# Attention backward for one cached token: outputs written over K and V, deeper pools, split head-0 columns, and weight reloads on another queue

## Chip, cores, metric

One core of one Trainium2 chip. A profile has its own span, about 2 us under the device time of the same run. The engines are PE (matrix products), DVE (vector), ACT (scalar), POOL (GpSimd) and SP, which here does nothing but issue DMAs. A DMA's data moves in packets on 16 DMA engines. dK, dV, dWo and dWq are the gradients of K, V, wo and wq.

## The reference, cut to what matters

The program is a forward pass and all its gradients. One token x (640 numbers) goes through an attention over a cached K and V (32 heads, 4096 positions, 128 wide) and through a small MLP, and a gate mixes the two.

```python
q = (x @ wq)                                   # 640 -> 32 heads x 128
p = softmax(einsum(q, k_cache) * Dh ** -0.5)   # per head, 4096 scores
a = einsum(p, v_cache) @ wo
b = mish(x @ w1 + b1) @ w2
out = g * a + (1 - g) * b                      # g = sigmoid(sum(x * gate_w))
# returned: out and the gradients of x, k_cache, v_cache, wq, wo, w1, b1, w2, gate_w
```

The gradients of K and V are outer products, as large as K and V. For each head the kernel reads 1 MiB of K and 1 MiB of V and writes 1 MiB of dK and 1 MiB of dV. With the weights and their gradients it reads 82.03 MB and writes 82.03 MB.

## The kernel before

The main loop has one `period` per head. SP issues all loads, POOL all large stores, each engine's own instructions run in program order.

```python
KB, VB = 4, 4
kv_in = ctx.enter_context(tc.tile_pool(name="kv_in", bufs=KB))
outs = ctx.enter_context(tc.tile_pool(name="outs", bufs=5))    # dK and dV
...
def load_k(h):                                 # load_v alike, bufs=VB
    kts[h] = kv_in.tile([P, J, Dh], BF16, name="Kn", tag="Kn", bufs=KB)
    nc.sync.dma_start(kts[h][:], Kv[h])
def load_wq(w):                                # two heads' groups, 1.25 MiB, two buffers
    wqs[w] = wts.tile([P, RC, WG * Dh], BF16, name="wq_g", tag="wq_g")
    nc.sync.dma_start(wqs[w][:], wq_v[:, :, w * WG * Dh:(w + 1) * WG * Dh])
def load_wo(g):                                # one group of four heads, 640 KiB, three buffers
    wos[g] = wts.tile([P, G, D], BF16, name="wo_g", tag="wo_g", bufs=3)
    nc.sync.dma_start(wos[g][:], wo_v[g])
...
load_wq(0); load_wo(0); load_k(0); load_v(0); load_k(1); load_v(1); load_wo(1)
# w1, b1, load_k(2), load_v(2), load_w2(0), load_w2(1)
...
def dwo():                                     # dWo is written over wo, then stored
    for i in range(G):
        nc.vector.tensor_scalar(wos[g][:, i, :], da_bc[:], fs["o4"][:, i:i + 1], None, ALU.mult)
    nc.gpsimd.dma_start(dwo_v[g], wos[g][:])
...
for h in range(H):
    hh, g = h % G, h // G
    if hh == 3:
        load_wo(g + 2)      # its buffer is free when group g-1's dWo store has landed
        if g % 2 == 0:
            load_wq(g // 2 + 1)
    load_k(h + 3)
    load_v(h + 3)
    if hh == 1 and g + 1 < NG:
        prep_steps(g + 1, h)          # q, dO and their columns for the next four heads
    period(h)
```

For head 0, `prep_steps(0, 0)` ran whole before the first score: q from wq, dO from wo, then the columns of both in one small matmul.

Of the kernel before, what the change touches and what calls it, by code (L numbers as in the profile page):

```python
# [10 lines left out]
F32 = mybir.dt.float32  # L11
BF16 = mybir.dt.bfloat16
# [4 lines left out]
def kernel(  # L17
# [24 lines left out]
    nc = tc.nc  # L42
    P = 128
    _, H, Sk, Dh = A_k_cache.shape
# [4 lines left out]
    G = 4  # L49
# [31 lines left out]
    out1_rows = out_1.rearrange("a b (c p) -> (a b c) p", p=P)  # L81
    out9_rows = out_9.rearrange("(c p) -> c p", p=P)

    KB, VB = 4, 4
    const = ctx.enter_context(tc.tile_pool(name="const", bufs=1))
    kv_in = ctx.enter_context(tc.tile_pool(name="kv_in", bufs=KB))
    outs = ctx.enter_context(tc.tile_pool(name="outs", bufs=5))
    tsb = ctx.enter_context(tc.tile_pool(name="tsb", bufs=4))
    wts = ctx.enter_context(tc.tile_pool(name="wts", bufs=2))
    small = ctx.enter_context(tc.tile_pool(name="small", bufs=3))  # L90
# [14 lines left out]


    vec_rows = const.tile([3 * RC, P], BF16, name="vec_rows")
    nc.scalar.dma_start(vec_rows[0:RC, :], x_rows)
    nc.scalar.dma_start(vec_rows[RC:2 * RC, :], dy_rows)
    nc.scalar.dma_start(vec_rows[2 * RC:3 * RC, :], gw_rows)  # L110

    kts, vts, wqs, wos = {}, {}, {}, {}

    def load_k(h):
        if h < H:
            kts[h] = kv_in.tile([P, J, Dh], BF16, name="Kn", tag="Kn", bufs=KB)
            nc.sync.dma_start(kts[h][:], Kv[h])
# [6 lines left out]
    def load_wq(w):  # L124
        if w < H // WG:
            wqs[w] = wts.tile([P, RC, WG * Dh], BF16, name="wq_g", tag="wq_g")
            nc.sync.dma_start(wqs[w][:], wq_v[:, :, w * WG * Dh:(w + 1) * WG * Dh])

    def load_wo(g):
        if g < NG:  # L130
            wos[g] = wts.tile([P, G, D], BF16, name="wo_g", tag="wo_g", bufs=3)
            nc.sync.dma_start(wos[g][:], wo_v[g])

    w2cs = {}

    def load_w2(c):
        w2cs[c] = mlp.tile([FP, FCC, D], BF16, name="w2c", tag="w2c", bufs=2)
        nc.sync.dma_start(w2cs[c][:], w2_v[:, c * FCC:(c + 1) * FCC, :])

    load_wq(0)  # L140
    load_wo(0)
    load_k(0)
    load_v(0)
    load_k(1)
    load_v(1)
# [6 lines left out]
    load_v(2)  # L152
    load_w2(0)
    load_w2(1)


    ident_f = const.tile([P, P], F32, name="ident_f")
# [79 lines left out]
    gps = {}  # L237
    steps, done = [], {}

    def add(name, kind, fn, deps=(), head=0):  # L240
        steps.append((name, kind, fn, tuple(deps), head))

    slot_no = [0]

    def slot(h, p=2, d=1):

        slot_no[0] += 1
        room = {"P": p, "D": d, "T": 99}
        for kind in ("T", "D", "P"):
            for st in list(steps):  # L250
                name, k, fn, deps, head = st
                if k != kind or head > h or not room[k]:
                    continue
                if all(done.get(x, 1 << 30) < slot_no[0] for x in deps):
                    fn()
                    done[name] = slot_no[0]
                    steps.remove(st)
                    room[k] -= 1

    def prep_steps(g, head):  # L260
# [13 lines left out]
        def do_part(i0, i1):  # L274
            def f():
                if i0 == 0:
                    gp["do4"] = small.tile([P, G], F32, name="do4", tag="do4")
                for i in range(i0, i1):
                    nc.vector.scalar_tensor_tensor(junk[:, 0:D], in0=wos[g][:, i, :], scalar=1.0, in1=da_bc[:],  # L279
                                                   op0=ALU.mult, op1=ALU.mult, accum_out=gp["do4"][:, i:i + 1])  # L280
                if i1 == G:
                    gp["do4b"] = small.tile([P, G], BF16, name="do4b", tag="do4b")
                    nc.vector.tensor_copy(gp["do4b"][:], gp["do4"][:])
            return f
# [15 lines left out]
                nc.tensor.matmul(dc_ps[:, hh:hh + 1], lhsT=gp["qd"][:, 1, hh * Dh:(hh + 1) * Dh],  # L300
                                 rhs=ident_bf[:, 0:1], start=True, stop=True)

        def m2():
            gp["m2"] = small.tile([P, 2, G, 2], BF16, name="m2", tag="m2")
            for w, src in ((0, gp["qc"]), (1, gp["dc"])):
                nc.vector.tensor_tensor(gp["m2"][:, w], src[:].unsqueeze(2).to_broadcast([P, G, 2]),
                                        mask2[:].to_broadcast([P, G, 2]), ALU.mult)

        def x2():
            x2 = gr_ps.tile([P, 2, G, 2], F32, name="x2_ps", tag="gr")  # L310
            nc.tensor.matmul(x2[:].rearrange("p a b c -> p (a b c)"), lhsT=sel2[:],
                             rhs=gp["m2"][:].rearrange("p a b c -> p (a b c)"), start=True, stop=True)
            t = gp["x2"] = qds[g % 3]
            hf = P // 2
            nc.scalar.mul(t[0:hf, :, :, :, 0], x2[0:hf], scale)
            nc.scalar.mul(t[hf:P, :, :, :, 1], x2[hf:P], scale)

        n = lambda x: f"{x}{g}"
        add(n("qcol"), "P", qcol, (), head)
        add(n("doa"), "D", do_part(0, 2), (), head)  # L320
        add(n("dob"), "D", do_part(2, 4), (n("doa"),), head)
        add(n("qbc"), "P", qbc, (n("qcol"),), head)
        add(n("dbc"), "P", dbc, (n("dob"), n("qbc")), head)
        add(n("dcol"), "P", dcol, (n("dbc"),), head)
        add(n("m2"), "T", m2, (n("dcol"),), head)
        add(n("x2"), "P", x2, (n("m2"),), head)


    o_all = const.tile([P, H], BF16, name="o_all")
# [2 lines left out]
    def finish_steps(g):  # L332
# [52 lines left out]
        add(n("o4c"), "T", o4c, (n("o4"),))  # L385
        add(n("amm"), "P", amm, (n("o4c"),))
        add(n("aadd"), "T", aadd, (n("amm"),))
        add(n("dwo"), "D", dwo, (n("aadd"),))
        for rc in range(RC):
            if g >= NG - 2:  # L390
                add(n(f"dx{rc}_"), "D", dx(rc, (g % 2) * GD, (g % 2 + 1) * GD, g - NG + 2 + NW - 1), (n("dqb"),))
            elif g % 2 == 1:
                add(n(f"dx{rc}_"), "D", dx(rc, 0, WG * Dh, g // 2), (n("dqb"),))


    def mlp_steps():
# [175 lines left out]
    def k_chunk(h, c, ts):  # L572
        ts.append(transposes(kts[h], c))

    def s_chunk(h, c, ts):
        gp = gps[h // G]
        if c == 0:
            sts[h] = {"A": sa_ps.tile([P, 512], F32, name="sA", tag="sA")}
        products(sts[h]["A"][:, 0:J + W], ts[c], c, gp["x2"][:, 0, h % G])

    def outer(dst, col, row, half):
# [8 lines left out]
    def dk_half(h, half):  # L590
        if h < 0:
            return
        st = sts[h]
        if half == 0:
            st["dK"] = outs.tile([P, J, Dh], BF16, name="dK_sb", tag="dVK")
        outer(st["dK"], st["ds"], gps[h // G]["qd"][:, 0, (h % G) * Dh:(h % G + 1) * Dh], half)
        if h == H - 1:
            a, b = half * (J // 2), (half + 1) * (J // 2)
            nc.gpsimd.dma_start(dKv[h][:, a:b, :], st["dK"][:, a:b, :])
        elif half == 1:  # L600
            nc.gpsimd.dma_start(dKv[h], st["dK"][:])  # L601
        if half == 1:
            sts.pop(h)

    def dv_half(h, half):
        st = sts[h]
        if half == 0:
            st["dV"] = outs.tile([P, J, Dh], BF16, name="dV_sb", tag="dVK")
        outer(st["dV"], st["p"], gps[h // G]["qd"][:, 1, (h % G) * Dh:(h % G + 1) * Dh], half)
        if half == 1:  # L610
            nc.gpsimd.dma_start(dVv[h], st["dV"][:])  # L611

    def period(h):
# [4 lines left out]
        S, Z, O, MM = A[:, 0:J], A[:, 96:96 + J], A[:, 128:128 + W], A[:, 256:384]  # L618
        B = st["B"] = sb_ps.tile([P, 512], F32, name="sB", tag="sB")
        DP, DQ, PT = B[:, 0:J + W], B[:, 128:128 + W], B[:, 256:384]  # L620
        vec = gp["x2"][:, 1, h % G]
        tv, tk = [], []
        V = lambda c: tv.append(transposes(vts[h], c))
# [62 lines left out]
        nc.scalar.copy(dq_all[:, h:h + 1], DQ[:, 0:1])  # L686
        if nxt:
            s_chunk(h + 1, 3, tk)
        kts.pop(h)
        vts.pop(h)  # L690
        slot(h, 2, 2)


# [2 lines left out]

    def dwq_make(rc):
        def f():
            t = dwqt[rc] = kv_in.tile([P, J * Dh], BF16, name="dwq_t", tag="Kn" if rc % 2 == 0 else "Vn", bufs=KB)
            nc.vector.tensor_scalar(t[:, 0:CL], dq_bc[:, 0:CL], x_f[:, rc:rc + 1], None, ALU.mult)  # L700
        return f

# [1 line left out]
        nc.gpsimd.dma_start(dwq_v[:, rc, 0:CL], dwqt[rc][:, 0:CL])  # L704

    prep_steps(0, 0)
    for _ in range(8):
        slot(0, 9, 9)
    tk = []
    for c in range(NT):  # L710
        k_chunk(0, c, tk)
        if c:
            s_chunk(0, c - 1, tk)
    s_chunk(0, NT - 1, tk)
    mlp_steps()
    for h in range(H):
        hh, g = h % G, h // G
        if hh == 3:
            assert g == 0 or f"dwo{g - 1}" in done
            load_wo(g + 2)  # L720
            if g % 2 == 0:
                assert g == 0 or f"dx{RC - 1}_{g - 1}" in done
                load_wq(g // 2 + 1)
        load_k(h + 3)
        load_v(h + 3)
        if hh == 1 and g + 1 < NG:
            rest = steps[:]
            steps.clear()
            prep_steps(g + 1, h)
            steps.extend(rest)  # L730
        if h == H - 3:
            for rc in range(RC):
                add(f"dwq{rc}", "D", dwq_make(rc), (f"dqb{NG - 2}",), h + (rc + 1) // 2)
                add(f"dwqs{rc}", "T", lambda rc=rc: dwq_store(rc), (f"dwq{rc}",), h)
        period(h)
        if hh == G - 1:
            mlp_left = steps[:]
            steps.clear()
            finish_steps(g)
            steps.extend(mlp_left)  # L740
# [79 lines left out]
```

## Time and profile before

| | before |
|---|---|
| median | 413.43 us (413.16 to 413.49) |
| span of the profile | 412.1 us |
| bytes moved | 164.93 MB, mean 400 GB/s |
| PE, DVE, ACT busy | 74%, 75%, 43% |

The table of 10-us windows of the kernel before, some of its rows. The columns are named in its first line; x counts instructions. The last two columns are the mean busy share of the 16 DMA engines (packets of two queues overlap a little, so a full engine shows 1.00 to 1.03) and what they moved.

```profile
core 0: us, PE busy (x) PEld busy (x) DVE busy (x) ACT busy (x) POOL busy (x), PEclk, DMA share, GB/s
0.00:10.00 10.00, 0.61 (x2) 0.28 (x2) 3.19 (x19) 1.66 (x3) 0.94 (x11) 1.00 0.80 288
...
30.00:40.00 10.00, 7.74 (x142) 6.95 (x141) 7.88 (x19) 4.57 (x11) 0.93 (x3) 0.92 1.01 315
...
190.00:200.00 10.00, 8.32 (x166) 7.42 (x165) 9.46 (x26) 5.12 (x12) 1.59 (x3) 1.00 1.02 425
...
250.00:260.00 10.00, 8.90 (x186) 7.77 (x185) 8.39 (x25) 6.64 (x14) 2.22 (x4) 1.00 1.02 418
260.00:270.00 10.00, 2.43 (x69) 2.13 (x65) 4.01 (x10) 1.77 (x5) 0.54 (x1) 0.85 1.02 421
...
370.00:380.00 10.00, 6.99 (x155) 6.43 (x154) 7.99 (x14) 4.60 (x11) 3.04 (x4) 1.00 0.93 384
380.00:390.00 10.00, 2.70 (x63) 2.04 (x61) 8.84 (x23) 0.53 (x2) 3.33 (x6) 0.65 1.01 418
...
400.00:410.00 10.00, 0.00 (x0) 0.00 (x0) 0.00 (x0) 0.00 (x0) 0.00 (x0) 0.50 0.05 19
```

DMA is full almost throughout. At 30 to 40 us it is busy and slow; at 400 to 410 us a share of 0.05 is about one engine of sixteen, still draining.

Three lines of the timeline of the kernel before follow: when wq's load was issued, when q was computed from it, and when head 0's dV was stored. A queue line (SPq) is the issue; the first number is its start.

```profile
0.74 0.46 SPq L127 DMA_DIRECT2D wq_g<-in_A_wq_dram  x1
...
11.25 0.67 PE L269 MATMUL qc_ps<-cols_bf,wq_g 128*128 128x1 bf16 x20
...
29.66 0.67 POOL L611 DMA_DIRECT2D out_dram<-dV_sb  x1 [28.10 <-DVE o_all L673]
```

The lists of waits (SP's own, then the computing engines'): who waited for what, total us, times, longest.

```profile
SPq L132 <- DMA out_dram<-wo_g: 62.9, 5, 17.7
PE qc_ps L269 <- DMA wq_g<-in_A_wq_dram: 11.5, 1, 11.5
```

SP waits 62.9 us in all before it may reload wo.

### The profile page before, as it was taken

To read this page: it belongs to the slowest core of one execution; us is meant where nothing else is said; L and a number is where in the kernel's file an instruction comes from. 1 tells how busy PE (TensorE), PEld (TensorE's weight loads), DVE (VectorE), ACT (ScalarE), POOL (GpSimd) and SP (SyncE) were. 2 spreads that over 40 slices of the span, in tenths; PEclk is the share of its full clock that TensorE was granted. 3 is DMA by queue.
4 is the path that set the end of the run, shared out by engine and by line. 5 is a ranking of instruction groups with operands and counts; after the bars stand their busy time and mean duration, and the time that the engine had idled before them with its cause. 6 is when DMAs were issued, how large, how long until landed. Compare 5 with 4: busy or idle time off the path is not lost.

```text
span 412.1 us, 13687 instructions
## 1 busy us (share of the span) xinstructions
PE 305.7 (74%) x5916; PEld 277.5 (67%) x5916; DVE 308.8 (75%) x807; ACT 177.0 (43%) x410; POOL 49.9 (12%) x95
## 2 busy tenths in 40 slices
PE   0688899988998789898977688439888788886200
PEld 0577888888887678787867687428777678775200
DVE  3338655685679999999897688528999997978840
ACT  1354534434445455445534356305554555543000
POOL 0001001111110111121111112001111111133310
PEclk9998999999999999989996899958999999999555
DMA  8999999999999999999999999999999999999970
GB/s 292 421 405 336 421 425 415 421 423 425 420 426 422 423 411 415 424 421 422 427 411 425 423 421 419 420 424 393 407 401 428 422 422 421 422 423 383 421 313 14
DMA packets 26328, 164.93 MB, mean 400 GB/s; under 512 B 2812, under 2 KB 2812, under 8 KB 10012
## 3 DMA queue, kind: packets, MB, share of 16 engines
q1 hardware_dynamic: 14116, 82.03, 48.8%
q0 software_dynamic: 12112, 82.03, 47.8%
q8 instruction: 46, 0.75, 0.7%
q14 instruction: 14, 0.11, 0.1%
q10 hardware_dynamic: 40, 0.01, 0.0%
HBM read 82.03 MB, written 82.03 MB: 398 GB/s over the span
## 4 chain that ended last, share of the span: by engine, by line
DVE 33%; PE 30%; DMA 23%; ACT 7%; issue 3%; ACTq 0%; DVEq 0%
DMA Kn<-in_A_k_cache_dram 17%; PE tr L559 10%; DVE dK_sb L584 8%; DVE dV_sb L584 7%; DMA out_dram<-dK_sb 6%; ACT tT L561 6%; PE sA L628 4%; DVE junk L376 4%; PE sA L568 3%; PE h_ps L407 3%; PE sB L681 3%; DVE junk L279 2%; DVE junk L508 2%; PE sB L568 1%; DMA vec_rows<-in_gate_w_dram 1%
## 5 line engine op out<-in xcount | busy, mean ns | idle before, releaser
L561 ACT COPY tT<-tr 128x512 f32<-128x512 f32 x256 | 142.3, 587 | 140.9 <-PE tr L559 140.2
L568 PEld LDWEIGHTS <-tT 128*128 128x128 bf16 x2048 | 80.4, 98 | 40.3 <-ACT tT L561 34.9
L559 PE MATMUL tr<-ident_f,Kn 128*128 128x128 f32 x512 | 80.7, 295 | 6.5 <-DMA Kn<-in_A_k_cache_dram 6.5
L584 DVE TENSOR_TENSOR dV_sb<-p_bf,qd 128x2048 bf16<-128x2048 bf16 x64 | 77.9, 1218 | 2.8 <-DMA out_dram<-dK_sb 2.8
L584 DVE TENSOR_TENSOR dK_sb<-ds_bf,qd 128x2048 bf16<-128x2048 bf16 x64 | 77.7, 1215 | 0.0
L559 PE MATMUL tr<-ident_f,Vn 128*128 128x128 f32 x512 | 72.6, 277 | 0.1
L568 PE MATMUL sA<-qd,tT 128*128 128x48 bf16 x1024 | 48.8, 187 | 23.5 <-ACT dq_all L686 12.8
L559 PEld LDWEIGHTS tr<-ident_f,Kn 128*128 128x128 f32 x512 | 60.1, 150 | 7.6 <-issue 6.2
L559 PEld LDWEIGHTS tr<-ident_f,Vn 128*128 128x128 f32 x512 | 56.8, 143 | 0.2 <-PE sA L568 0.2
L568 PE MATMUL sB<-qd,tT 128*128 128x48 bf16 x1024 | 46.1, 183 | 0.1
L611 POOL DMA_DIRECT2D out_dram<-dV_sb x32 | 18.3, 572 | 166.8 <-DVE dV_sb L584 74.2
L628 PEld LDWEIGHTS <-Vn 128*128 128x128 bf16 x1024 | 30.2, 96 | 10.4 <-issue 10.4
L601 POOL DMA_DIRECT2D out_dram<-dK_sb x31 | 18.3, 591 | 151.0 <-DVE rz L650 77.7
L628 PE MATMUL sA<-e_bf,Vn 128*128 128x48 bf16 x1024 | 30.7, 183 | 7.6 <-DVE zs L648 6.0
L681 PE MATMUL sB<-ds_bf,Kn 128*128 128x48 bf16 x1024 | 31.8, 185 | 3.5 <-DVE ds_bf L670 3.5
L681 PEld LDWEIGHTS <-Kn 128*128 128x128 bf16 x1024 | 29.2, 97 | 3.8 <-issue 3.8
L632 DVE TENSOR_REDUCE m<-sA 128x1 f32<-128x32 f32 x32 | 6.0, 189 | 31.3 <-PE sA L568 25.6
L279 DVE SCALAR_TENSOR_TENSOR junk<-wo_g,da_bc 128x640 bf16<-128x640 bf16 x32 | 26.3, 821 | 2.6 <-ACT da_bc L220 1.1
L376 DVE SCALAR_TENSOR_TENSOR junk<-wq_g,dq_bc 128x1024 bf16<-128x1024 bf16 (+1 forms) x25 | 25.1, 1004 | 0.2
L668 DVE TENSOR_SCALAR_CACHE_REDUCE dj<-sB,rz 128x128 f32<-128x128 f32 x32 | 11.1, 346 | 11.2 <-PE sB L662 11.2
L407 PE MATMUL h_ps<-cols_bf,w_sb 128*96 128x1 bf16 x90 | 18.2, 313 | 1.4 <-ACT qd L290 0.7
L407 PEld LDWEIGHTS <-w_sb 128*96 128x96 bf16 x90 | 17.6, 272 | 1.8 <-issue 0.7
(144 smaller groups left out, 283.8 us busy)
## 6 DMA issues: line engine op xcount, KB each, us to landing
Kn<-in_A_k_cache_dram SPq DMA_DIRECT2D x32, 1024.0 KB, 27.2
Vn<-in_A_v_cache_dram SPq DMA_DIRECT2D x32, 1024.0 KB, 26.9
out_dram<-dV_sb POOLq DMA_DIRECT2D x32, 1024.0 KB, 12.2
out_dram<-dK_sb POOLq DMA_DIRECT2D x31, 1024.0 KB, 12.3
wq_g<-in_A_wq_dram SPq DMA_DIRECT2D x4, 1280.0 KB, 19.0
wo_g<-in_A_wo_dram SPq DMA_DIRECT2D x8, 640.0 KB, 13.3
out_dram<-wo_g POOLq DMA_DIRECT2D x8, 640.0 KB, 11.6
out_dram<-dwq_t POOLq DMA_DIRECT2D x5, 896.0 KB, 16.6
```

What stands on the lines that cost most here:

```text
L279: nc.vector.scalar_tensor_tensor(junk[:, 0:D], in0=wos[g][:, i, :], scalar=1.0, in1=da_bc[:], op0=ALU.mult, op1=ALU.mult, accum_out=gp["do ...
L376: nc.vector.scalar_tensor_tensor(junk[:, c0:c1], in0=wqs[w][:, rc, c0:c1], scalar=1.0, in1=dq_bc[:, w * WG * Dh + c0:w * WG * Dh + c1], op ...
L407: nc.tensor.matmul(hps[a][:, fc:fc + 1], lhsT=w1_sb[:, rc, :].rearrange("p (q c) -> p q c", c=FCN)[:, :, fc], rhs=x_bf[:, rc:rc + 1], star ...
L559: nc.tensor.transpose(tp[:, t, :], flat[:, k * P:(k + 1) * P], ident_f[:])
L561: nc.scalar.copy(sb[:].rearrange("p a b -> p (a b)"), tp[:].rearrange("p a b -> p (a b)"))
L568: nc.tensor.matmul(out[:, 2 * k:2 * k + W], lhsT=tb[:, t, par, :], rhs=vec[:, par, :].unsqueeze(1).to_broadcast([P, W // 2, 2]), start=(pa ...
L584: nc.vector.tensor_tensor(dst[:, a:b, :].rearrange("p j (a b) -> p j a b", b=2), col[:, a:b, :].unsqueeze(2).to_broadcast([P, n, Dh // 2, 2]),
L601: nc.gpsimd.dma_start(dKv[h], st["dK"][:])
L611: nc.gpsimd.dma_start(dVv[h], st["dV"][:])
L628: nc.tensor.matmul(O, lhsT=vts[h][:, j, :], rhs=st["e"][:, j:j + 1].to_broadcast([P, W]), start=(j == 0), stop=(j == J - 1))
L668: nc.vector.tensor_scalar(dj[:], PT, rz[:], None, ALU.mult, ALU.add, accum_out=dd[:])
L681: nc.tensor.matmul(DQ, lhsT=kts[h][:, j, :], rhs=ds[:, j, 0:1].to_broadcast([P, W]), start=(j == 0), stop=(j == J - 1))
```

## The change

The intent: give PE and DVE more heads of K and V in hand, at the same SBUF size (13 tiles of 1 MiB before and after), by writing dK over K and dV over V. Keep the weights from standing behind that longer line of K and V loads by reloading them from ACT. Start head 0's scores when q is there, without the dO columns. The diff, cut:

```diff
-    KB, VB = 4, 4
+    KB, VB = 7, 6
-    outs = ctx.enter_context(tc.tile_pool(name="outs", bufs=5))
-    nc.scalar.dma_start(vec_rows[0:RC, :], x_rows)          # and two more
+    nc.sync.dma_start(vec_rows[0:RC, :], x_rows)
     def load_wq(w):
-            nc.sync.dma_start(wqs[w][:], ...)
+            (nc.scalar if w else nc.gpsimd).dma_start(wqs[w][:], ...)
     def load_wo(g):
-            nc.sync.dma_start(wos[g][:], wo_v[g])
+            (nc.sync if g < 2 else nc.scalar).dma_start(wos[g][:], wo_v[g])
     # load_w2: sync for c < 2, scalar after
     load_wq(0)
+    load_k(0)
     load_wo(0)
-    load_k(0)
     ...
+    for i in range(3, VB - 1):          # heads 3 and 4, and K of head 5, up front
+        load_k(i); load_v(i)
+    load_k(VB - 1)
-            st["dK"] = outs.tile([P, J, Dh], BF16, name="dK_sb", tag="dVK")
+            st["dK"] = kts.pop(h)       # dV alike: vts.pop(h)
     # prep: m2 and x2 split into a q part and a dO part; head 0 runs k_chunk / s_chunk
     # between the q part and the rest; dWo and dx steps go ahead of the next group's prep
     for h in range(H):
+        if hh == 2 and g % 2 == 0:
+            load_wq(g // 2 + 1)
         if hh == 3:
             load_wo(g + 2)
-            if g % 2 == 0:
-                load_wq(g // 2 + 1)
-        load_k(h + 3)
-        load_v(h + 3)
+        load_v(h + VB - 1)
+        if h:
+            load_k(h + KB - 2)
```

More of the change, by code (lines that the diff above doesn't have):

```diff
@@ L107 @@
     vec_rows = const.tile([3 * RC, P], BF16, name="vec_rows")
-    nc.scalar.dma_start(vec_rows[0:RC, :], x_rows)
-    nc.scalar.dma_start(vec_rows[RC:2 * RC, :], dy_rows)
-    nc.scalar.dma_start(vec_rows[2 * RC:3 * RC, :], gw_rows)
+    nc.sync.dma_start(vec_rows[0:RC, :], x_rows)
+    nc.sync.dma_start(vec_rows[RC:2 * RC, :], dy_rows)
+    nc.sync.dma_start(vec_rows[2 * RC:3 * RC, :], gw_rows)
     kts, vts, wqs, wos = {}, {}, {}, {}
@@ L126, in load_wq @@
             wqs[w] = wts.tile([P, RC, WG * Dh], BF16, name="wq_g", tag="wq_g")
-            nc.sync.dma_start(wqs[w][:], wq_v[:, :, w * WG * Dh:(w + 1) * WG * Dh])
+            (nc.scalar if w else nc.gpsimd).dma_start(wqs[w][:], wq_v[:, :, w * WG * Dh:(w + 1) * WG * Dh])
     def load_wo(g):
@@ L137, in load_w2 @@
         w2cs[c] = mlp.tile([FP, FCC, D], BF16, name="w2c", tag="w2c", bufs=2)
-        nc.sync.dma_start(w2cs[c][:], w2_v[:, c * FCC:(c + 1) * FCC, :])
+        (nc.sync if c < 2 else nc.scalar).dma_start(w2cs[c][:], w2_v[:, c * FCC:(c + 1) * FCC, :])
     load_wq(0)
+    load_k(0)
     load_wo(0)
-    load_k(0)
     load_v(0)
@@ L154 @@
     load_w2(1)
+    for i in range(3, VB - 1):
+        load_k(i)
+        load_v(i)
+    load_k(VB - 1)
     ident_f = const.tile([P, P], F32, name="ident_f")
@@ L238, with add @@
     steps, done = [], {}
-    def add(name, kind, fn, deps=(), head=0):
-        steps.append((name, kind, fn, tuple(deps), head))
+    def add(name, kind, fn, deps=(), head=0, first=False):
+        steps.append((name, kind, fn, tuple(deps), head, first))
     slot_no = [0]
@@ L250, in slot @@
             for st in list(steps):
-                name, k, fn, deps, head = st
+                name, k, fn, deps, head, _ = st
                 if k != kind or head > h or not room[k]:
@@ L301, in dcol, with m2, f, x2 @@
                                  rhs=ident_bf[:, 0:1], start=True, stop=True)
-        def m2():
-            gp["m2"] = small.tile([P, 2, G, 2], BF16, name="m2", tag="m2")
-            for w, src in ((0, gp["qc"]), (1, gp["dc"])):
+        def m2(w):
+            def f():
+                if w == 0:
+                    gp["m2"] = small.tile([P, 2, G, 2], BF16, name="m2", tag="m2")
+                src = gp["dc"] if w else gp["qc"]
                 nc.vector.tensor_tensor(gp["m2"][:, w], src[:].unsqueeze(2).to_broadcast([P, G, 2]),
                                         mask2[:].to_broadcast([P, G, 2]), ALU.mult)
-        def x2():
-            x2 = gr_ps.tile([P, 2, G, 2], F32, name="x2_ps", tag="gr")
-            nc.tensor.matmul(x2[:].rearrange("p a b c -> p (a b c)"), lhsT=sel2[:],
-                             rhs=gp["m2"][:].rearrange("p a b c -> p (a b c)"), start=True, stop=True)
-            t = gp["x2"] = qds[g % 3]
-            hf = P // 2
-            nc.scalar.mul(t[0:hf, :, :, :, 0], x2[0:hf], scale)
-            nc.scalar.mul(t[hf:P, :, :, :, 1], x2[hf:P], scale)
+            return f
+        def x2(w):
+            def f():
+                x2 = gr_ps.tile([P, G, 2], F32, name="x2_ps", tag="gr")
+                nc.tensor.matmul(x2[:].rearrange("p b c -> p (b c)"), lhsT=sel2[:],
+                                 rhs=gp["m2"][:, w].rearrange("p b c -> p (b c)"), start=True, stop=True)
+                t = gp["x2"] = qds[g % 3]
+                hf = P // 2
+                nc.scalar.mul(t[0:hf, w, :, :, 0], x2[0:hf], scale)
+                nc.scalar.mul(t[hf:P, w, :, :, 1], x2[hf:P], scale)
+                gp[f"x{w}"] = True
+            return f
         n = lambda x: f"{x}{g}"
         add(n("qcol"), "P", qcol, (), head)
+        add(n("m2q"), "T", m2(0), (n("qcol"),), head)
+        add(n("x2q"), "P", x2(0), (n("m2q"),), head)
         add(n("doa"), "D", do_part(0, 2), (), head)
@@ L324, in prep_steps @@
         add(n("dcol"), "P", dcol, (n("dbc"),), head)
-        add(n("m2"), "T", m2, (n("dcol"),), head)
-        add(n("x2"), "P", x2, (n("m2"),), head)
+        add(n("m2d"), "T", m2(1), (n("dcol"),), head)
+        add(n("x2d"), "P", x2(1), (n("m2d"),), head)
     o_all = const.tile([P, H], BF16, name="o_all")
@@ L387, in finish_steps @@
         add(n("aadd"), "T", aadd, (n("amm"),))
-        add(n("dwo"), "D", dwo, (n("aadd"),))
+        add(n("dwo"), "D", dwo, (n("aadd"),), first=True)
         for rc in range(RC):
@@ L392, in finish_steps @@
             elif g % 2 == 1:
-                add(n(f"dx{rc}_"), "D", dx(rc, 0, WG * Dh, g // 2), (n("dqb"),))
+                add(n(f"dx{rc}_"), "D", dx(rc, 0, WG * Dh, g // 2), (n("dqb"),), first=True)
     def mlp_steps():
@@ L578, in s_chunk @@
             sts[h] = {"A": sa_ps.tile([P, 512], F32, name="sA", tag="sA")}
+        assert gp["x0"]
         products(sts[h]["A"][:, 0:J + W], ts[c], c, gp["x2"][:, 0, h % G])
@@ L607, in dv_half @@
         if half == 0:
-            st["dV"] = outs.tile([P, J, Dh], BF16, name="dV_sb", tag="dVK")
+            st["dV"] = vts.pop(h)
         outer(st["dV"], st["p"], gps[h // G]["qd"][:, 1, (h % G) * Dh:(h % G + 1) * Dh], half)
@@ L620, in period @@
         DP, DQ, PT = B[:, 0:J + W], B[:, 128:128 + W], B[:, 256:384]
+        assert gp["x1"]
         vec = gp["x2"][:, 1, h % G]
@@ L688, in period @@
             s_chunk(h + 1, 3, tk)
-        kts.pop(h)
-        vts.pop(h)
         slot(h, 2, 2)
@@ L698, in f @@
         def f():
-            t = dwqt[rc] = kv_in.tile([P, J * Dh], BF16, name="dwq_t", tag="Kn" if rc % 2 == 0 else "Vn", bufs=KB)
+            t = dwqt[rc] = kv_in.tile([P, J * Dh], BF16, name="dwq_t", tag="Vn" if rc % 2 else "Kn",
+                                      bufs=VB if rc % 2 else KB)
             nc.vector.tensor_scalar(t[:, 0:CL], dq_bc[:, 0:CL], x_f[:, rc:rc + 1], None, ALU.mult)
@@ L706 @@
     prep_steps(0, 0)
-    for _ in range(8):
-        slot(0, 9, 9)
-    tk = []
-    for c in range(NT):
-        k_chunk(0, c, tk)
-        if c:
-            s_chunk(0, c - 1, tk)
-    s_chunk(0, NT - 1, tk)
+    tk = []
+    slot(0, 1, 1)
+    k_chunk(0, 0, tk)
+    slot(0, 1, 1)
+    k_chunk(0, 1, tk)
+    slot(0, 1, 1)
+    for c in range(1, NT):
+        if c > 1:
+            k_chunk(0, c, tk)
+        s_chunk(0, c - 1, tk)
+    s_chunk(0, NT - 1, tk)
+    while steps:
+        slot(0, 9, 9)
     mlp_steps()
@@ L717 @@
         hh, g = h % G, h // G
+        if hh == 2 and g % 2 == 0:
+            assert g == 0 or f"dx{RC - 1}_{g - 1}" in done
+            load_wq(g // 2 + 1)
         if hh == 3:
@@ L720 @@
             load_wo(g + 2)
-            if g % 2 == 0:
-                assert g == 0 or f"dx{RC - 1}_{g - 1}" in done
-                load_wq(g // 2 + 1)
-        load_k(h + 3)
-        load_v(h + 3)
+        load_v(h + VB - 1)
+        if h:
+            load_k(h + KB - 2)
         if hh == 1 and g + 1 < NG:
-            rest = steps[:]
-            steps.clear()
+            ahead = [st for st in steps if st[5]]
+            rest = [st for st in steps if not st[5]]
+            steps[:] = ahead
             prep_steps(g + 1, h)
```

## The prediction

> **What bounds it now.** The DMA engines. The table of windows of 10 us has their mean busy share at 0.99 to 1.03 from 10 to 370 us, 415 to 427 GB/s in most windows. The kernel moves 164.93 MB; at 423 GB/s, the steady rate there, that is 390 us of the 412.1 us span (estimate). The rest: first weight packets at 1.9 us; 0 to 10 us runs at 288 GB/s; 30 to 40 us at 315 GB/s although the engines are busy, because the first two w2 chunks load slowly there (their 7680 B packets took 479 ns each, the third chunk's, at 208 to 226 us, 298 ns); and after 400 us one of 16 engines still drains stores alone, to 407.9 us (25 GB/s in the DMA view's slices), then 4 us to the end.
>
> Compute is close behind: PE and DVE are busy 75% each, DVE 9.4 to 9.9 of 10 us in most windows of 120 to 210 and 290 to 340 us. PE starves only in 210 to 280 us (2.4 and 4.9 us busy in 260 to 280; the chain has K loads of 34.7 and 33.6 us), some 15 us in all. DMA stays full then, so that starvation is the DMA bound showing through, not a separate cost.
>
> **What the change does.**
> - K and V deeper (7 and 6 for 4 and 4), outputs in place of five output buffers: the same 13 MB. Removes DVE's 2.8 us wait for an output buffer and most starvation of PE. No byte goes away, so a full DMA gains nothing.
> - Weights on ACT's ring. The Trainium skill, "DMA: Bandwidth & Descriptors", section "Issuing engines are not separate DMA queues", says they share the same 16 engines; this trace agrees so far (share 1.0 with one load ring). ACT now waits for the dWo store before it reloads wo (SP's waits there: five of 9.5 to 17.7 us); the reload comes one period (10 to 12 us) after the store's issue, so I expect about 1 us, five or six times, mostly absorbed.
> - Columns apart: head 0's scores need q only. Before, they wait for the dO columns (x2 at 17.2 us) though wq landed at 7.0. wq now shares the engines with K0 and lands near 9 to 10 us; head 0's period starts about 6 us earlier, the first dV store is issued near 24 us for 29.7. Stores then run beside the w2 loads, as they did beside the third chunk: most of the 2.6 us lost in 30 to 40 us comes back, about 2 us.
> - wq from POOL, vec_rows ahead of K0 on SP: DMA fills about 0.5 us later.
>
> **On the critical path:** -2 us (w2), -0.5 to -1 (small DMA gaps at 278 to 284 and 374 to 378 us), +0.5 (start). The straggling engine's work stays. Sum: 413.4 - 2 - 1 + 0.5, about 411.
>
> **Predicted: 411 us, 8 in 10 between 404 and 417.** Faster by over 2%: 0.15; within 2%: 0.76; slower: 0.09.
>
> **What shows it.** Right: DMA share about 1.0 through 370 us; 30 to 40 us near 420 GB/s; first dV store near 24 us; PE's hole at 260 to 280 us smaller or moved, the time not following; the lone engine's tail of some 7 us still there. Wrong: DMA share under 0.95 for long; ACT waiting over 15 us in all on dWo stores.
>
> **What would make it wrong.** Faster: the straggler's lag is not its own work but comes from the w2 loads or ring sharing, and shrinks: up to 7 us more. Slower: loads run so far ahead that the end is compute-bound, DMA half idle; or ACT's waits hold PE up.

## More of the kernel before

The metric is the device time of one execution in microseconds (us).

PE's hole at 260 to 270 us is a wait for the reload of wq, which PE needs next in its program (11.5 us, to 274.1 us), while DMA stays full.

SP computes nothing, so nothing but its own loads stops with it. Those loads can come late, though: the wq reload behind PE's hole was issued at 242.4 us, right after SP's wait for a dWo store that took 20.2 us to land.

## The result, and the profile after

| | before | after |
|---|---|---|
| median of four runs | 413.46 us (413.16 to 413.77) | 417.91 us (417.47 to 418.78) |
| span of the profile | 412.1 us | 415.3 us |
| last store issued | 393.5 us | 401.9 us |
| 15 of 16 engines done with that store | 400.5 us | 411.0 us |
| last engine done with it | 407.9 us | 411.0 us |

The ratio is 1.011, 95% interval 1.0091 to 1.0129. Ratios here are the mean time of one kernel's fast runs over that of the other's of the same rounds, so not quite the ratio of the medians. The last two rows come from the times at which each engine's share of that store landed.

The same windows of the kernel after:

```profile
0.00:10.00 10.00, 1.86 (x12) 1.27 (x12) 3.20 (x19) 2.51 (x5) 1.97 (x12) 1.00 0.72 263
...
30.00:40.00 10.00, 8.34 (x182) 7.96 (x182) 7.92 (x20) 4.53 (x12) 1.13 (x2) 0.96 1.01 328
...
190.00:200.00 10.00, 4.60 (x86) 4.00 (x86) 6.78 (x16) 2.13 (x7) 1.07 (x2) 0.98 1.02 424
...
250.00:260.00 10.00, 1.77 (x26) 1.71 (x27) 0.00 (x0) 2.00 (x5) 0.00 (x0) 0.54 1.02 427
260.00:270.00 10.00, 8.80 (x183) 8.08 (x180) 9.06 (x26) 5.48 (x14) 0.62 (x2) 0.95 0.79 329
...
370.00:380.00 10.00, 8.83 (x192) 7.94 (x192) 9.47 (x25) 5.37 (x12) 1.96 (x3) 1.00 0.85 343
380.00:390.00 10.00, 8.36 (x179) 7.70 (x179) 8.98 (x20) 5.05 (x12) 4.00 (x6) 1.00 0.81 332
...
400.00:410.00 10.00, 0.72 (x2) 0.27 (x2) 6.75 (x28) 0.26 (x1) 1.48 (x2) 0.50 0.94 384
```

There are new holes in PE and DVE at 190 to 200 and 250 to 260 us. DVE did nothing at all in the second. DMA carries on through the holes with loads, then runs short at 260 to 270 us (0.79), where no new stores have come and the loads are far ahead. At 370 to 390 us compute still works at full speed, DVE about 9 of 10 us, and DMA waits for it (0.85, 0.81): the end is bound by compute.

The timeline of the kernel after, the lines that answer to the three of before:

```profile
1.29 1.01 POOL L126 DMA_DIRECT2D wq_g<-in_A_wq_dram  x1 [0.85 <-POOLq L823]
...
15.00 0.69 PE L272 MATMUL qc_ps<-cols_bf,wq_g 128*128 128x1 bf16 x20 [6.77 <-DMA wq_g<-in_A_wq_dram]
...
31.58 0.58 POOL L623 DMA_DIRECT2D out_dram<-Vn  x1 [28.44 <-DVE o_all L686]
```

q is computed 3.75 us later than before, because wq lands at 15.0 us and not at 7.0. (In before q did not wait for wq: PE's program had another product first, ready at 10.0 us.) The first dV store is 1.9 us later, though the scores no longer wait for dO.

The hole at 190 to 200 us, in the timeline of ACT in the kernel after:

```profile
193.79 0.18 ACT L323 ACTIVATE qd<-x_ps 64x8 bf16<-64x8 f32 x1
200.35 0.34 ACTq L131 DMA_DIRECT2D wo_g<-in_A_wo_dram  x1
201.06 1.07 ACT L572 COPY tT<-tr 128x512 f32<-128x512 f32 x2 [7.09 <-DMA out_dram<-wo_g]
```

ACT has nothing else in its way: it stands at the wo reload until the dWo store, issued at 183.2 us, has landed at 200.3. Behind it stand the copies of PE's transposes, so PE stops, and DVE with it. The list of waits of the kernel after sums this up, and shows SP's waits, which are now for stores of dV:

```profile
ACT tT L572 <- DMA out_dram<-wo_g: 31.8, 4, 14.0
...
SPq L121 <- DMA out_dram<-Vn: 248.4, 24, 20.7
```

Where the time went, in one sum. Fifteen engines finish 10.5 us later (411.0 for 400.5). Added up over all packets of loads and stores, an engine's packet time, the mean of the 16, is 402.1 us for 398.5, so about 3.6 us is slower packets. The rest, about 6.9 us, is idleness; by their shares, the four windows with a low one (0 to 10, 260 to 270, 370 to 390 us) hold 5.9 us of it more than before. Against that, the lone engine's 7.4 us of drain at the end of before (407.9 less 400.5) is gone. That it caught up in DMA's gaps fits, but the trace does not tell the engines apart. 10.5 less 7.4 is the 3.1 us by which the last landing moved.

### The profile page after: what moved, and what is told of

It is laid out like the page before. It is cut to its first block, busy times and chain, and to the rows that moved or that the text cites. A ratio compares the mean times of both kernels' runs of the same rounds, so it can differ in the third digit from the quotient of the medians.

```text
span 415.3 us, 13795 instructions
## 1 busy us (share of the span) xinstructions
PE 307.6 (74%) x5924; PEld 279.7 (67%) x5924; DVE 308.3 (74%) x807; ACT 178.9 (43%) x426; POOL 50.8 (12%) x96
## 4 chain that ended last, share of the span: by engine, by line
issue 33%; DMA 25%; DVE 21%; PE 12%; POOL 4%; ACT 3%; POOLq 0%; ACTq 0%; DVEq 0%
DMA out_dram<-wo_g 13%; DVE Kn L596 6%; DMA wo_g<-in_A_wo_dram 5%; DVE Vn L596 4%; PE tr L570 4%; DMA wq_g<-in_A_wq_dram 3%; ACT tT L572 3%; DMA Vn<-in_A_v_cache_dram 3%; DVE junk L387 3%; PE sA L641 2%; POOL out_dram L623 2%; POOL out_dram L613 2%; PE sA L579 2%; DVE junk L519 1%; PE sB L694 1%
## 5 line engine op out<-in xcount | busy, mean ns | idle before, releaser
L596 DVE TENSOR_TENSOR Vn<-p_bf,qd 128x2048 bf16<-128x2048 bf16 x64 | 78.0, 1218 | 0.0
L596 DVE TENSOR_TENSOR Kn<-ds_bf,qd 128x2048 bf16<-128x2048 bf16 x64 | 77.7, 1215 | 0.0
L570 PE MATMUL tr<-ident_f,Vn 128*128 128x128 f32 x512 | 74.3, 281 | 0.0
L579 PE MATMUL sB<-qd,tT 128*128 128x48 bf16 x1024 | 47.6, 187 | 27.9 <-ACT tT L572 27.8
L570 PEld LDWEIGHTS tr<-ident_f,Vn 128*128 128x128 f32 x512 | 57.9, 145 | 0.3 <-issue 0.3
L623 POOL DMA_DIRECT2D out_dram<-Vn x32 | 18.2, 568 | 184.4 <-DVE Vn L596 66.3
L641 PEld LDWEIGHTS <-Vn 128*128 128x128 bf16 x1024 | 31.8, 98 | 8.7 <-issue 8.4
L641 PE MATMUL sA<-e_bf,Vn 128*128 128x48 bf16 x1024 | 32.3, 186 | 6.0 <-DVE zs L661 4.6
L613 POOL DMA_DIRECT2D out_dram<-Kn x31 | 18.2, 586 | 144.4 <-DVE rz L663 68.1
L661 DVE TENSOR_REDUCE zs<-sA 128x1 f32<-128x32 f32 x32 | 6.0, 187 | 32.4 <-PE sA L659 31.8
L645 DVE TENSOR_REDUCE m<-sA 128x1 f32<-128x32 f32 x32 | 6.0, 188 | 22.1 <-PE sA L579 14.2
```

The source lines that it names most:

```text
L570: nc.tensor.transpose(tp[:, t, :], flat[:, k * P:(k + 1) * P], ident_f[:])
L579: nc.tensor.matmul(out[:, 2 * k:2 * k + W], lhsT=tb[:, t, par, :], rhs=vec[:, par, :].unsqueeze(1).to_broadcast([P, W // 2, 2]), start=(pa ...
L596: nc.vector.tensor_tensor(dst[:, a:b, :].rearrange("p j (a b) -> p j a b", b=2), col[:, a:b, :].unsqueeze(2).to_broadcast([P, n, Dh // 2, 2]),
L613: nc.gpsimd.dma_start(dKv[h], st["dK"][:])
L623: nc.gpsimd.dma_start(dVv[h], st["dV"][:])
L641: nc.tensor.matmul(O, lhsT=vts[h][:, j, :], rhs=st["e"][:, j:j + 1].to_broadcast([P, W]), start=(j == 0), stop=(j == J - 1))
```

## The experiments

There were three theories, and more than one can hold. A: the reloads on ACT stop ACT, in program order, until dWo stores land. B: the start, with wq from POOL. C: K and V loads run so far ahead that something else pays for it. Each run went with runs of before on the same chip; ratios are to those. Times of a kernel vary by up to 4 us between runs in some of these (the intervals show it). "Wait on dWo" means the wait for a dWo store to land, after which the buffer may be reloaded.

### Weights back on SP

```diff
-            (nc.scalar if w else nc.gpsimd).dma_start(wqs[w][:], ...)
+            (nc.sync if w else nc.gpsimd).dma_start(wqs[w][:], ...)
-            (nc.sync if g < 2 else nc.scalar).dma_start(wos[g][:], wo_v[g])
+            nc.sync.dma_start(wos[g][:], wo_v[g])              # w2 alike
```

> The kernel after, with the later reloads of wq, wo and w2 issued from SP again; all else as after. Theory A (ACT waits in order for the dWo stores, 31.8 us in four waits, and PE stops with it): ACT's waits on dWo stores vanish, PE's holes at 190 to 205, 240 to 260 and 300 to 307 us close, the DMA gap at 260 to 270 us (329 GB/s) goes; 413 to 415 us, against 417.9 of after. Rival B (the slow start, wq from POOL landing at 15.0 us): no change in time, 417 to 418.5 us. Rival C (deep pools and outputs in place: loads run ahead of compute and the end is bound by compute): holes go, but the time stays within 1 us of after, as the gap moves to the end.

Measured (run 1): 419.48 us, ratio 1.0135 (1.0122 to 1.0148). Theory A's number was missed by 5 us, on the wrong side of after. ACT's waits went, but another wait took their place, in the list of waits of this run:

```profile
DVE junk L282 <- DMA wo_g<-in_A_wo_dram: 33.1, 3, 18.6
```

On SP the reloads stand in line behind five heads of K and V, and DVE waits for wo. PE waited too, 13.6 us for a K load. So this run moved the stall and did not test A.

### The start of before

```diff
-            (nc.scalar if w else nc.gpsimd).dma_start(wqs[w][:], ...)
+            (nc.scalar if w else nc.sync).dma_start(wqs[w][:], ...)
-    nc.sync.dma_start(vec_rows[0:RC, :], x_rows)               # and two more
+    nc.scalar.dma_start(vec_rows[0:RC, :], x_rows)
```

> The kernel after, with wq's first load issued first on SP and vec_rows on ACT, as in before; the reloads stay on ACT's ring. Rival B: wq lands near 7 us, the first dV store is issued near 23 us for 31.6, and the time falls by 2 to 4 us, to 414 to 416. Theory A: the start is earlier as B says, but the time falls by at most 1 us, as the waits of ACT stay.

Measured (run 2): 416.64 us, ratio 1.0066 (1.0054 to 1.0078), 0.44% under after's ratio. wq landed at 7.1 us, the first dV store was issued at 26.4 us, and 30 to 40 us ran at 399 GB/s, the w2 packets at 310 ns. B holds for about 1.8 us.

This profile must not be taken for the start alone. Nine profiles have this start, with q at 11.1 to 11.4 us, and their first dV store was issued at 26.4 to 30.3 us; in the five with the start of after it was 31.6 to 34.0. The spread comes from PE: four transposes took 1.1 us at first and 0.6 us after a switch, with the granted clock at 1.00 on both sides, and the switch came by 15 us in this run and after 25 in the third. What sets it is not shown. In the profiles with w2 in this place and POOL storing, the w2 packets follow the time at which that store's first packet moved: 310 ns here, with 30.4 us, 414 to 421 ns with 32.9 to 33.5 us, and 461 to 498 ns with 35.4 us or later. So the prediction's chain from early stores to faster w2 loads holds; that the start makes the stores early enough is luck in part.

### Both at once

> Both edits together: all weights on SP, wq first. What is left of the change is the split of the columns, and the deep pools with outputs in place. Theory A with B adding: 410 to 413 us, about as before or 1 to 2 us under it. Theory C: no better than 414 us, slower than before, with DMA share under 0.9 in 370 to 390 us.

Measured (run 3): 417.18 us, ratio 1.0062 (1.0042 to 1.0082). This is what C expected: no better than 414 us, and the DMA share was 0.75 at 370 to 380 us; A and B together had expected 410 to 413. Against the first run, which differs by the start alone, it is 0.73% less. From the list of waits:

```profile
DVE junk L282 <- DMA wo_g<-in_A_wo_dram: 30.1, 2, 17.8
```

### wo reloaded one period later, from ACT

```diff
         if hh == 3:
-            load_wo(g + 2)
+            if g == 0:
+                load_wo(2)
+        if hh == 0 and g > 1:
+            load_wo(g + 1)
```

> The kernel after, with wo reloaded one period later, still from ACT: the dWo store has then had about 22 us to land, so ACT hardly waits, while the ring is the same. Theory A (the wait, not the ring): ACT's waits on dWo stores under 5 us in all, 413 to 415 us, as the run with the weights on SP. If a third ring in itself is what costs: no change, 417 to 418.5 us.

Measured (run 4): 416.42 us, ratio 1.0059 (1.0047 to 1.0071), 0.51% under after's. ACT's waits on dWo fell to 14.2 us, not under 5, and one of 4.8 us for the w2 store came. The time is above A's 413 to 415 us. So taking away about half the wait gave about 2 us: A has a part in it, less than expected. The lone engine's drain was back (7.7 us), as DMA had fewer gaps.

### The start and the later reload together

> The two edits that each gave about 2 us, together: the kernel after with wq first on SP and vec_rows on ACT, and wo reloaded one period later from ACT. If the start (1.9 us by the second run) and ACT's waits on dWo stores (2.1 us by the fourth) are separate costs and together make up the loss: 413.5 to 414.8 us, level with before. If they overlap, or a third part (loads running far ahead, buffers held until the store lands) costs as well: 415 to 417 us.

Measured (run 5): 416.04 us, ratio 1.0036 (1.0009 to 1.0063), runs from 413.66 to 417.48. Added up, the two gains would give 1.0015, which lies inside the interval, and 14.2 us of ACT's waits are still there. So the run does not decide whether there is a third part.

### K and V three heads ahead in the program, all weights on SP

```diff
-    for i in range(3, VB - 1):
-        load_k(i); load_v(i)
-    load_k(VB - 1)
...
-        load_v(h + VB - 1)
-        if h:
-            load_k(h + KB - 2)
+        load_k(h + 3)
+        load_v(h + 3)
```

This is on top of the run with both edits undone, so the pools of seven and six and the outputs in place stay.

> As the third run (all weights on SP, wq first), with K and V loaded three heads ahead as in before, in place of five; pools of seven and six and outputs in place stay, so a load never waits for a store. Theory C (running far ahead is what costs: weights queue behind the K and V loads, and loading ends with compute far behind): DVE's waits on wo and PE's on wq go (30.1 and 4.9 us in the third run), the gap of 370 to 390 us shrinks, time 411 to 414 us, 3 us or more under the third run. If outputs in place are what costs (buffers held until the store has landed): no gain, 416 us or more.

Measured (run 6): 413.08 us, ratio 0.9977 (0.9959 to 0.9996). That is 0.85% under the run with five heads ahead (1.0062), and the first arrangement of the change that is a little faster than before. Waits of DVE on wo and of PE on later wq loads are gone. SP's own waits, in this run:

```profile
SPq L131 <- DMA out_dram<-wo_g: 82.0, 5, 23.3
SPq L126 <- DVE junk L383: 24.9, 2, 18.1
```

SP now waits where ACT did, at no cost that the time shows. The outputs in place and the deep pools are therefore not what costs.

### Stores on SP, loads on ACT

> As the run before, with dK's and dV's stores issued from SP and the K and V loads from head 3 on from ACT, so that POOL's queue carries only the small weight gradients. It asks where the straggling engine comes from, which in before drains alone for 7.4 us at the end. If it comes from POOL's queue: the lag of the last engine falls under 3 us although DMA is full, and the time falls to 405 to 410 us. If it comes from something else (the instruction fetches): the lag stays at 6 to 8 us, the time within 2 us of the run before.

Edit: in the run before, dK's and dV's stores `nc.gpsimd` to `nc.sync`, K and V loads from head 3 on `nc.sync` to `nc.scalar`. Measured (run 7): 416.04 us, ratio 1.0049 (1.0036 to 1.0061). The last engine's lag was 6.6 us on SP's last store, so POOL's queue of K and V stores is not the lone engine's cause. The time itself says little, as ACT again waited in order for buffers (11.2 us for dK stores).

### Before, with w2 loaded at head 3

> The kernel before, with the first two w2 chunks loaded at head 3 instead of up front, so that stores run beside them. The prediction's term: their packets fall from 479 to about 300 ns, 30 to 40 us run near 420 GB/s, and the time falls by about 2 us, to 411.5 to 412.5. Rival: the slow stretch is not w2's own, other loads are as slow there when the stores begin: 30 to 40 us still near 320 GB/s, no change in time.

Measured (run 8): 413.99 us, ratio 0.9991 (0.9979 to 1.0003). 30 to 40 us ran at 423 GB/s as expected, but the w2 packets were slow again in their new place, 417 ns at 64 to 75 us. In that stretch the stores paused (almost none moved at 69 to 72 us). The slow stretch had moved with w2, and no time was won.

### After, three heads ahead and nothing else

> The kernel after with one edit: K and V loaded three heads ahead, not five. The start (wq from POOL) and the reloads from ACT stay. Theory C (running far ahead is the root): ACT's waits on dWo stores shrink with it (31.8 us in after), loading ends with less compute left, and the time falls by 2 to 3.5 us to 414.5 to 416; what remains over before is the start (about 1.9 us). Rival: the waits of ACT and the start are the whole loss and the depth matters only with weights on SP: within 1 us of after, 417 to 418.5 us.

Measured (run 9): 419.31 us, ratio 1.0132 (1.0108 to 1.0156). C as I had put it fell here: the edit alone gave nothing. ACT's waits on dWo stayed at 31.6 us, and SP's waits show why:

```profile
SPq L116 <- DMA out_dram<-Kn: 139.7, 22, 13.8
SPq L121 <- DMA out_dram<-Vn: 114.9, 23, 7.6
```

SP's waits are almost all for buffers. With seven and six of them it runs on to the same loads whatever the place of the load in the program's loop: it issued most K loads four or five heads beyond the one whose dV was next to be stored, and in after mostly four. "Three ahead" changes only the order within SP's line, and that matters only where the weights stand in the same line. So what the sixth run did was to put the weights two heads earlier in the line, and to let SP's wait for a dWo store hold the K and V loads back.

### Four heads ahead, all weights on SP

> The run with three heads ahead and all weights on SP (413.1 us), with four heads ahead; five gave 417.2. Theory C, a graded cost: 414 to 416 us, with waits on wo and wq in between. Rival: the step from four to five is where loads begin to wait for stores, so all the cost sits there: 412.5 to 413.5 us.

The sixth run's kernel, with four heads ahead. Measured (run 10): 414.79 us, ratio 1.0016 (1.0004 to 1.0028). Five, four and three heads give 1.0062, 1.0016 and 0.9977: graded. DVE's waits on wo were 24.3 us in two.

### Before, with the reloads on ACT

> The kernel before, with only the reloads of wq, wo and w2 moved to ACT's ring. If ACT's waits on dWo stores cost by themselves, also at three heads ahead: waits of ACT over 15 us in all and 415 to 417 us. If they matter only with deep prefetch, where the store takes longer to land: waits under 10 us, time within 1 us of before.

Measured (run 11): 428.74 us, ratio 1.0354 (1.0325 to 1.0384), far outside both expectations. ACT did not wait for dWo at all. PE waited for wq:

```profile
PE qc_ps L269 <- DMA wq_g<-in_A_wq_dram: 24.6, 3, 12.4
```

ACT issues a load when its own program gets there; SP had been there long before. ACT issued the three wq reloads at 54.6, 158.9 and 265.5 us, SP in before at 43.6, 148.9 and 242.4. The first landed at about 92 us for 75. While PE waits no buffer comes free, and DMA runs dry too: 372 GB/s over 120 to 200 us for 420 in before.

### Three heads ahead, w2 after head 3's K and V

```diff
-    load_w2(0)                    # up front
-    load_w2(1)
...
         load_k(h + 3)
         load_v(h + 3)
+        if h == 0:
+            load_w2(0)
+            load_w2(1)
```

> The run with three heads ahead (413.1 us), with the first two w2 chunks loaded after head 3's K and V, so that they move at about 36 to 42 us beside stores. If w2's packets are slow only where no stores run: their mean falls from about 470 to about 300 ns, 30 to 40 us run over 400 GB/s, no other slow stretch appears, 410.5 to 411.5 us. Rival (the lone engine's drain at the end takes up what is won, or the slow stretch moves as in the eighth run): 412.5 to 413.5 us.

Measured (run 12): 412.09 us, ratio 0.9953 (0.994 to 0.9966): faster than before and after, by 0.5% and by 1.6% (0.9953 over 1.011). The w2 packets took 308 ns for 461 in the sixth run. The windows of 30 to 40 us, first of the sixth run, then of this one:

```profile
30.00:40.00 10.00, 8.37 (x183) 7.75 (x182) 8.30 (x21) 5.33 (x13) 1.52 (x3) 1.00 1.02 327
```

```profile
30.00:40.00 10.00, 8.82 (x194) 8.19 (x193) 9.52 (x25) 5.64 (x15) 1.07 (x2) 1.00 1.01 422
```

The packet time of an engine fell from 397.5 to 395.5 us, so the prediction's 2 us for w2 are there in the packets, where stores do run beside. The run's time fell by 1.0 us, or 0.24%, which is barely clear of the noise; the expectation had been 410.5 to 411.5 us.

### Three heads ahead, with the start of after

> The run with three heads ahead and all reloads on SP (413.1 us), with wq's first load from POOL and vec_rows on SP, as in after. If the start is a cost of its own: first dV store near 32 to 34 us for 29.8, 415 to 416 us. Rival: DMA is full all the same, and the start is made up later: 412.5 to 413.8 us.

Measured (run 13): 416.18 us, ratio 1.0042 (1.003 to 1.0054). Against the sixth run (0.9977) the start alone costs 0.65%, 2.7 us. wq landed at 14.8 us, the first dV store was issued at 33.4 us. The start is not made up later.

The same run settles more, set beside the ninth, which differs from it only in that ACT issues the reloads: 1.0132 there, 1.0042 here, so ACT's issuing costs 0.9% (3.7 us) at three heads ahead. At five heads ahead the same swap gained nothing (1.0110 with ACT, 1.0135 with SP). Each edit alone leaves a stall, ACT's wait for a dWo store or DVE's for wo, and only both together remove it:

| start of after (wq from POOL) | reloads on ACT | reloads on SP |
|---|---|---|
| five heads ahead | 1.0110 (after) | 1.0135 (run 1) |
| three heads ahead | 1.0132 (run 9) | 1.0042 (run 13) |

### Four wo buffers

This is the second run's kernel with a fourth wo buffer. The fourth buffer fits only with one V buffer less.

```diff
-    KB, VB = 7, 6
+    KB, VB = 7, 5                 # and K of head 5 loaded up front
-            wos[g] = wts.tile(..., tag="wo_g", bufs=3)
+            wos[g] = wts.tile(..., tag="wo_g", bufs=4)
```

> The kernel after with the start of before, four wo buffers for three and five V buffers for six: the buffer that ACT reloads was stored a whole group earlier. Theory A (ACT's in-order wait for the dWo store is the cost beside the start): no wait of ACT on dWo stores, 412 to 414 us. If ACT's ring in itself costs, or loads running ahead in deep pools: 415 to 417 us although the waits are gone.

Measured (run 16): 415.67 us, ratio 1.0028 (0.9997 to 1.006), runs from 412.72 to 416.95. ACT's waits on dWo stores are gone (one of 5.5 us for the w2 store stays). The time lies in the range expected if more than the waits costs (415 to 417 us), not in A's 412 to 414. Against the second run (1.0066), which has the same start and the waits, it is 0.38% less, with an uncertainty of about 0.34%, and the edit also takes a V buffer away. So this run's estimate for A is about 1.6 us, loosely known, and 0.5% is left to the sixth run.

> The run before with the first two w2 chunks loaded last of the first loads, where stores already run: their packets near 300 ns, and 1.5 to 2 us under the run before, 410.5 to 412.5 us. Rival: what is won early is lost to the lone engine's drain or to ACT's wait for the w2 store: within 0.7 us of the run before.

The same with w2 last of the first loads (run 17): 414.65 us, ratio 1.0011 (0.9988 to 1.0034). The w2 packets took 301 ns; the gain of 1.0 us against the run before, where 1.5 to 2 were expected, is within the spread.

## Why the prediction was wrong, point by point

The measured 417.91 us lies above the range (404 to 417). Not one cause but three terms of the sum failed, the first three points.

1. **The start.** The failed step reads "wq now shares the engines with K0 and lands near 9 to 10 us; head 0's period starts about 6 us earlier, the first dV store is issued near 24 us". wq landed at 15.0 us and the first store was issued at 31.6. Issued from POOL at 1.29 us, wq's first packet moved only at 5.3 us; from SP in before, 1.1 us after the issue. After that it shared with K, wo and V, as I had said. I had booked +0.5 us for it; undone alone it gave 0.44% (1.8 us) in the second run and 0.73% between the first and third, and put into the sixth run it cost 0.65% (2.7 us). Even with wq at 7 us the step was too hopeful: the first store came at 26.4 to 30.3 us, with PE at its slower rate for a part of the start that differs between profiles, and its first packet moved another 4 to 6 us after the issue (35.4 us in before, 37.0 in after).
2. **The w2 loads.** The step "most of the 2.6 us lost in 30 to 40 us comes back, about 2 us" hung on step 1. In after those packets took 461 ns for 479, and nothing came back. The mechanism was right: 310 ns in the second run, where the stores moved from 30.4 us, and 0.24% between the sixth and the twelfth run.
3. **ACT's wait.** The step "I expect about 1 us, five or six times, mostly absorbed" was mis-sized. ACT waited 31.8 us in four waits, the longest 14.0. ACT came to the reload about 10.3 us after the store's issue (73.1 us of landing less 31.8 of waits, over four), as the step had it. What it had wrong is the landing: in before 10.9 to 11.7 us for most dWo stores, one of 20.2; in after the four that mattered took 14.3, 17.2, 25.2 and 16.4 us. Why they took longer is not shown. The wait was not absorbed, because PE's transposes wait for ACT's copies. With the waits removed the ratio fell by 0.38%; at three heads ahead, with the reloads given to SP, by 0.9%.
4. **"Loads run so far ahead that the end is compute-bound"** was named as what would make it wrong on the slow side, and it is what the end of after shows. It fits 1 and 3: compute lost 8.4 us (last store issued at 401.9 for 393.5), while DMA used the holes to load ahead and had nothing left to do at 370 to 390 us.
5. **"The straggling engine's work stays"** was wrong for after: its lag was 0.0 us at the end. In the kernels with DMA full to the end it was there again (7.0 to 8.0 us in the sixth, twelfth and sixteenth runs). Here a lone engine's lag was a cost only while the others had few gaps.
6. What was right: DMA is the bound in before, deeper pools do not pay by themselves, and moving weights to another queue adds no bandwidth. PE's starvation in before was misread: the chain shows a K load of 33.6 us, but the hole at 262.6 to 274.1 us ended with the wq reload, and that was late through SP's wait for a dWo store. The conclusion stood, as DMA stayed full (share 1.02).

The runs account for the loss: giving the reloads to SP at three heads ahead takes after from 1.0110 to 1.0042, and the start of before takes that to 0.9977. What stays open: how the 0.5% between the four-buffer run and the sixth run divides (deep K and V loads, the place of the weights, or one V buffer less); what sets PE's switch to its faster rate at the start; and where the lone engine comes from. The 3.6 us of slower packets in after are shown, not explained: at 269 to 276 us 8192 B load packets took 426 ns in the mean, for a usual 309.

## What to carry to other kernels

A load's issuing queue decides more than bandwidth: an engine that computes issues the load only when its program gets there and stops at it until the buffer is free, while an idle issuer runs ahead as far as buffers allow. When loads share one queue, the depth of the bulk stream sets how late the small urgent loads behind it land, so place the weights by when they are needed and not by where the loop happens to stand. And before crediting an earlier start, check which queue feeds the first operand and when its first packet really moves.

## What the Trainium skill lacked or had wrong

- "DMA: Bandwidth & Descriptors", section "Issuing engines are not separate DMA queues", says that issuing from several engines "will only save the time on the sequencer it takes to initiate the DMA". The bandwidth part agrees: the DMA share was 1.02 with three queues as with two. The section has no figure for what in-order waits and later issue on a compute engine cost: moving three weights' reloads from SP to ACT, and nothing else, made the kernel before 3.5% slower (428.74 us, by later issue) and run 9, with 31.6 us of waits for dWo stores, 0.9% slower than run 13.
- The same page, section "Specifications", gives a first byte at about 1 us from GpSimd and about 0.6 us from SP or ACT. Here the first packet came 4.0 us after POOL's first issue started (1.29 to 5.3 us), and 1.1 us after SP's (0.74 to 1.88 us). The first dV store's packets came 5.8 us after its issue in before (29.66 to 35.41 us).
- The same page, section "Latency and other measured facts", guesses that two slower engines owe it to GpSimd's descriptor rings. One engine did lag (7.4 us at the end of before), but with all dK and dV stores issued from SP it still lagged 6.6 us. The trace does not number the engines, so whether it is one of those two is not shown.
- "SBUF — State Buffer", section "Door 1: The DMA port swizzle (why `[64,N]` ≈ `[32,N]`)", bears on loads that fill only some partitions, but has no row for 96 partitions and nothing on such a load beside stores. Here w2, loaded into 96 partitions from SP, took 461 to 498 ns for a 7680 B packet where no or few stores ran, and 293 to 310 ns beside a steady stream of stores; K's and V's 8192 B packets into 128 partitions took 310 to 311 ns either way in before (10 to 28 us, 40 to 240 us). Whether the 96 partitions are the reason was not tested.
